# Packing w_in's 64-row remainder of two items into the two row halves of TensorE, in a three-stage kernel on one core

## The chip, the cores and the metric

The kernel runs on one NeuronCore of a Trainium2 chip. The metric is the device time of one execution in microseconds; the kernel before took 1141.08 us (median of three runs, 1140.94 to 1141.94). Engines are named as in the profile: PE multiplies, PEld is its weight loading, DVE, ACT and POOL work element by element, SP issues the DMAs.

## What is computed

Two sequences of 4096 tokens with 192 channels go through a dynamic convolution (per token and head a softmax over 7 taps, applied to the token and the six before it) and then two feed-forward layers over all 8192 tokens:

```python
out = np.einsum('bshk,bskhg->bshg', softmax(weight_gen), windows_of(x))   # -> (8192, 192)

h = x @ w_in                       # 192 -> 2048
g = where(h >= 1, h, where(h <= -1, 0, (h + 1) ** 2 / 4))
x = g @ w_out                      # 2048 -> 192

h = x @ w_in2
g = h - tanh(h)
return g @ w_out2
```

All is float32. To use TensorE at its faster float32r format, each operand is split into a high part, the value rounded to that format, and a low part, the rest; a product is then high x high + low x high + high x low.

## The kernel before

The 8192 tokens are 16 blocks (b) of N = 512, the 2048 hidden channels 16 chunks (f) of P = 128. An **item** (m, b, f) is chunk f of block b in feed-forward layer m (0 or 1): a first product into one PSUM bank h (`item`, L850; contracted over 192 channels), an activation on ACT and DVE (L880 to L901), a cast of the result to its high part gh on ACT (L918) and a low part gl on DVE or POOL (L926), and a second product with w_out's chunk f into the block's accumulators, three items later. `order` (L287) lists the 512 items: first the blocks (0, 0) and (0, 1) interleaved, the second SKEW items behind the first, then (0, 2), then (1, 0) and (1, 1) interleaved, then (0, 3), (1, 2), (0, 4), (1, 3) and so on, one whole block after the other, to (1, 15).

192 channels are 128 + 64. The first 128 fill TensorE's rows; the last 64, called the third part here, fill half of them. Weights come as float32 and are split on the chip (`weights`, L316): per group of two items a load, two steps that take the bits apart (ACT and ACT or POOL), a `join` on DVE (L357), a cast to the high part on ACT (L374) and the low part on DVE or POOL (L378). For w_in such a group is 512 words wide: 2 x 128 columns of the first 128 channels, and 2 x 128 columns of the third part, which is loaded twice, into rows 0 to 63 and again into rows 64 to 127. The activations (tile xt, named a for layer 0, b for layer 1) have the high part of the first 128 channels, their low part, and in a third plane the third part's high in rows 0 to 63 and its low in rows 64 to 127.

**Plain items** (all of the first LANES = 64 items, and the last block): the first product is five full-row matmuls of 512 columns, `mm1` (L860, matmul at L864): high x high, low x high and high x low of the first 128 channels, then w_in's third part, high and low, against the plane that has high and low side by side. The second product is five full-row matmuls (L939 to L946), in the last block a form with the tokens on the other side (L951).

**Paired items** (from item 64 to the last block): `both` (L816) runs the first product of two items and the second product of two earlier ones as 64-row matmuls, always one on rows 0 to 63 beside one on rows 64 to 127 (`chunks`, L782; `second`, L764; `weave`, L793). There the third part needs its high part in both halves; a copy of it is made by ACT (L1038, L1135) or by a further DMA (L701) into tiles x3.

The first items' second product takes the joined weights without splitting, in plain float32 (`whole`, L309; L905 to L912): items 0 to 3 of block (0, 0) and item 0 of block (0, 1), by WHOLE = (4, 1).

The convolution of blocks 0 to 2 ends on PE with transposes and is then split by ACT and DVE (`conv`, L398; hi1 at L625, lo1 at L631). From block 3 on the rows go out to DRAM and come back transposed (`move_rows`, L655; `back`, L686). Between layer 0 and layer 1 `finish1` (L1017) splits a block's result.

No engine's order is written by hand: `Plan.run` (L70) lays every task in time by keys and assumed durations and writes the instructions in that order. The keys' offsets are the constants from L1172 on.

Of the kernel before, what the change touches and what calls it, by code (L numbers as in the profile page):

```python
# [169 lines left out]
def tile_dynconv_moe_moe(  # L170
# [45 lines left out]

    ident = const.tile([P, P], F32, tag="ident", name="ident")
# [9 lines left out]
    win = tiles("win", 2, [P, 4, FF], F32R)  # L227
# [8 lines left out]
    x3_t = {}  # L236

    def x3(s):

        n, k = divmod(s.n, 2)  # L240
        if n not in x3_t:
            x3_t[n] = const.tile([P, 2, N], F32R, tag=f"raw{n}", name=f"x3_{n}")
        return x3_t[n][D1:P, k]

    def third(m, b):

        s = x3_of[m, b]
        return xt_t[s.n][D1:P, b] if m and b < 2 else x3(s)

    def xt_tile(s, name, shape=(P, 3, N), dt=F32R):  # L250
        xt_t[s.n] = const.tile(list(shape), dt, tag=f"xt{s.n}", name=name)
# [5 lines left out]
    def bits(w):  # L257
# [9 lines left out]
        "x3": [4, 5, 6, 7],  # L267
# [20 lines left out]
    for first, second, skew in turns:  # L288
        if first == (1, 0):
            order += [(0, 2, f) for f in range(NF)]  # L290
        order += [(*first, f) for f in range(skew)]
        step = 1 if first == (0, 0) else 2
        for f in range(0, NF, step):
            order += [(*second, f + k) for k in range(step)]
            order += [(*first, skew + f + k) for k in range(step) if skew + f + k < NF]
# [20 lines left out]
    def weights(kind, m, c, lead):  # L316

        key = at[m, 0, 2 * c] - lead + kind * KOFF
        n = 2 * D if kind else 2 * WC
# [10 lines left out]
        def load(e):  # L330
            r = raws[raw.n]
            if kind == 0:
                w = bits_in[m][:, c * WC:(c + 1) * WC]
                return [e.dma_start(r[q], w[k]) for q, k in (
                    ((slice(0, P), slice(0, WC)), slice(0, P)), ((slice(0, D1), slice(WC, None)), slice(P, D)), ((slice(D1, P), slice(WC, None)), slice(P, D)),
                )]
            else:
                return e.dma_start(r[:, 0:n].rearrange("p (f c) two -> p f c two", f=2), bits_out[m][:, 2 * c:2 * c + 2])
# [23 lines left out]
        def pieces():  # L362
            src = value().rearrange("p (a c) -> p a c", a=2)
            if kind == 0:
                cs = slice(c * WC, (c + 1) * WC)
                return [(win[m][:, 0:2, cs], win[m][:, 2:4, cs], src)]
            w = wout[m][:, 2 * c:2 * c + 2, :]

            return [
                (w[:, :, P:2 * P], w[:, :, 0:P], src[:, :, 0:P]),  # L370
                (w[:, :, 2 * P:2 * P + D1], w[:, :, 2 * P + D1:], src[:, :, P:D]),
            ]

        def cast(e):  # L374
            for hi, lo, src in pieces():
                e.copy(hi, src)
# [11 lines left out]
        t = wcast[kind, m, c] = plan.add(on("ACT", 0.09 + 0.43 * k + 0.1 * split), key2, cast, [t], uses=[val])  # L388
# [6 lines left out]
    a_of, b_of, x3_of = {}, {}, {}  # L395
    x3_free = []

    def conv(b, banks, base, gap):  # L398
# [216 lines left out]
        def parts():  # L615

            xtr = X(2).rearrange("p (q h n) -> p q h n", h=2, n=P)
            if b == 0:
                p1r = p1.rearrange("p (q h n) -> p q h n", h=2, n=P)
                sides = p1r[:, :, 0], p1r[:, :, 1]  # L620
            else:
                sides = (p1[:, 0:N // 2].rearrange("p (q n) -> p q n", n=P),) * 2
            return [(slice(0, D1), slice(D1, P), sides[0], xtr[:, :, 0]), (slice(D1, P), slice(0, D1), sides[1], xtr[:, :, 1])]

        def hi1(e):  # L625
            if b == 0:
                xt_tile(xt, f"a_{b}")
            for u, _, p, s in parts():
                e.copy(s[u], p[u])

        def lo1(e):  # L631
            for u, v, p, s in parts():
                e.tensor_tensor(s[v], p[u], s[u].bitcast(F32), op=ALU.subtract)
# [8 lines left out]
        if b == 0:  # L642
            h1 = plan.add(on("ACT", 0.76), last, hi1, [tr1], takes=[xt], uses=second_)
# [3 lines left out]
        else:  # L647
            h0 = plan.add(on("ACT", 0.48), last, hi0, [tr], takes=[xt], uses=first_)
            h1 = plan.add(on("ACT", 0.76), last, hi1, [h0], uses=second_ + [xt])
            l0 = plan.add(on("DVE", 0.60), last, low0, [h0], uses=first_ + [xt])  # L650
            l1 = plan.add(on("DVE", 0.86), last, lo1, [h1], uses=second_ + [xt])
        marks["evac", b] = l1
        xdone[0, b] = [h0, h1, l0, l1]

    def move_rows(b, wg, xw, mem, xt, dep, key, turn):  # L655
# [21 lines left out]
        xs3 = x3_of[0, b] = slot("x3")  # L677
# [8 lines left out]
        def back(e, n, k):  # L686
# [19 lines left out]
        for n, k in ((0, 0), (0, 1), (1, 0), (1, 1)):  # L706
            first = [] if moves else [marks["fin1", b - 1]]
            moves.append(plan.add(
                on("DMA", 1.0), last, lambda e, n=n, k=k: back(e, n, k), [d1 if n else d0] + moves[:1] + first + (x3_free if len(moves) == 1 else []),
                takes=[xs3] if len(moves) == 1 else [] if moves else [xt], uses=[spot] + ([xt] if moves else []), late=3.0,  # L710
# [21 lines left out]
    head, ending, closes = [], [], []  # L732
    lows, apart = slot("xt"), slot("bank", lambda: (0, 1, 6, 7))

    def paired(m, b):

        return b >= MOVED - m and (m, b) != (1, NB - 1)
# [9 lines left out]
    HALVES = [slice(0, D1), slice(D1, P)]  # L747
# [33 lines left out]

    def chunks(lane, m, b, f, h, xs):  # L782

        rs, fs = HALVES[lane], slice(f * P, (f + 1) * P)
        ops = [(0, 0), (2, 0), (0, 1), (1, 2)] + ([(3, 2 + lane)] if f % 2 == lane else [])

        def mm(e, n, k, c):
            x = third(m, b) if c == 3 else xt_t[xs.n][rs, c]
            return e.matmul(ps[h.n], win[m][rs, k, fs], x, start=lane == 0 and n == 0, stop=lane == 1 and n == len(ops) - 1)  # L789

        return [lambda e, n=n, k=k, c=c: mm(e, n, k, c) for n, (k, c) in enumerate(ops)]

# [23 lines left out]
    def both(m, b, f, h0, h1, need):  # L816
# [25 lines left out]
        t = plan.add(on("PE", 0.68), i, one, need + [last[0]] + late2[g0][9], takes=[h0, h1] + opens, uses=[xs, x3_of[m, b]] + rest, late=0.0)  # L842
        t = plan.add(on("PE", 1.365), i, two, [t] + late2[g1][9], uses=[h0, h1, xs, x3_of[m, b]] + both_, late=0.0)
        first = plan.add(on("PE", 0.2265 * n), i, three, [t], uses=[h0, xs, x3_of[m, b]] + both_, late=0.35)
        end = last[0] = plan.add(on("PE", 0.2265 * (10 - n)), i + 1, four, [first], uses=[h1, xs, x3_of[m, b]] + both_, late=0.35)
# [4 lines left out]
    def item(m, b, f, after):  # L850
# [9 lines left out]
        def mm1(e, ns=range(5)):  # L860
            w, xt = win[m], xt_t[xs.n]
            for n in ns:
                k, c = [(0, 0), (2, 0), (0, 1), (1, 2), (3, 2)][n]
                e.matmul(ps[h.n], w[:, k, fs], xt[:, c], start=n == 0, stop=n == (2 if i < 2 else 4))  # L864

        need1 = after + xdone[m, b] + [wdone.get((0, m, f // 2))]
        if i < 2:
            head.append(plan.add(on("PE", 0.46), i - 1.5, lambda e: mm1(e, range(2)), xdone[m, b][:1] + need1[-1:] + head, takes=[h], uses=[xs], late=0.1))
            first = plan.add(on("PE", 0.68), i, lambda e: mm1(e, (3, 4, 2)), need1 + head[:1], uses=[h, xs], late=0.35)
        elif not lanes1(i):  # L870
            first = plan.add(on("PE", 1.135), i, mm1, need1, takes=[h], uses=[xs], late=0.35)
        elif f % 2 == 0:
            h1 = slot("bank", h_banks(m, b))
            first, second = both(m, b, f, h, h1, need1)
# [53 lines left out]
        tlo = plan.add(engines, i, low_part, [thi], takes=[gl], uses=[g], lock=True)  # L928
# [81 lines left out]
    held, thirds = [], []  # L1010
# [6 lines left out]
    def finish1(b, acc, key, t, g=None):  # L1017
# [14 lines left out]
        rl = plan.add(on("DVE", 0.60), key, lambda e: e.tensor_tensor(X(2)[D1:P], M(), X(2)[0:D1].bitcast(F32), op=ALU.subtract), [rh], uses=[s, tm])  # L1032
        marks["fin1", b] = r
        hold(g, [(h1, "gh", 4), (r, "gl", 5), (h0, "gh", 5), (l0, "gl", 6), (rh, "gh", 6), (rl, "gl", 7)])
        xdone[1, b] = [h0, l0, rh, rl]
        if paired(1, b):
            s3 = x3_of[1, b] = slot("x3")
            xdone[1, b].append(plan.add(on("ACT", 0.525), key, lambda e: e.copy(x3(s3), X(2)[0:D1]), [rh] + x3_free, takes=[s3], uses=[s]))  # L1038
# [81 lines left out]
    x3_free += [wdone[kind, 1, c] for kind in range(2) for c in range(NF // 2)]  # L1120
    place = {q: n for n, q in enumerate(streams)}
    for m, b, f in order:
# [6 lines left out]
        if (m, b, f) == (1, 0, 0):  # L1129
            s3 = slot("xt")  # L1130

            def copy3(e, c):
                if c == 0:
                    xt_tile(s3, "thirds")
                e.copy(xt_t[s3.n][D1:P, c], xt_t[b_of[c].n][0:D1, 2])  # L1135

            for c in range(2):
                x3_of[1, c] = s3
                t = plan.add(on("ACT", 0.525), LANES - 7.0, lambda e, c=c: copy3(e, c), [xdone[1, c][2]] + thirds[:1], takes=[] if c else [s3], uses=[b_of[c]] + ([s3] if c else []))
                thirds.append(t)  # L1140
# [8 lines left out]
        if m and b < 2 and lanes1(at[m, b, f]):  # L1149
            dep = dep + [thirds[b]]  # L1150
        if at[m, b, f] == LANES:
            dep = dep + [prev2.get((1, 0)), prev2.get((1, 1))]
# [20 lines left out]
WHOLE = (4, 1)  # L1173
LEAD2 = 4.0
DONE1, DONE2 = 9.0, 11.0
FLEX = 2.0
WARM = 24
VONE = 1
KOFF = 4.0
LOAD1 = 4.0  # L1180
LOWF = 4.0
UNTIL = 3.5
SKEW = 11
LANES = 64
SKEW2 = 8
RAMP, RAMP_UNTIL = 0.5, 48
BASE3, BASE = 40.0, 40.0
PACE = 1.3
LEAD = (4.0, 14.0)
CONV1 = (0.0, 0.5)  # L1190
# [30 lines left out]
```

## Time and profile before

| | us |
|---|---|
| median of three runs | 1141.08 |
| span of the profiled execution | 1138.7 |
| PE busy in it | 1132.1 |
| DVE busy | 974.1 |
| ACT busy | 843.7 |
| POOL busy | 109.1 |

The span runs from the first to the last instruction of the profiled execution; its time outside the span isn't recorded, and the median of the unprofiled runs lies 2.4 us above the span. TensorE's granted clock is 1.0 of full speed in every stretch, that is 2.4 GHz, but for 0.99 in the last 29 us.

How to read it: a matmul's duration in the trace (0.39 us here) is longer than the distance to the next one, since matmuls are pipelined; the distance of two starts is what a matmul costs PE. 64*128 in a row is a matmul on 64 rows, 128*128 one on all rows.

### The profile page before, as it was taken

How to read it: one execution, taken by the hardware profiler on the slowest of the kernel's cores; microseconds unless marked ns; L12 is line 12 of the kernel's file. 1: busy time of each engine (PE TensorE's matmuls, PEld its weight loads, DVE VectorE, ACT ScalarE, POOL GpSimd, SP SyncE). 2: the span in 40 equal slices, each digit the busy share in tenths (PEclk: the TensorE clock that was granted, in tenths of full speed). 3: DMA queues.
4: the chain of work that ended last, by engine and by line, in shares of the span. 5: the costliest groups of instructions: out<-in, count | busy, mean ns of one | idle time of the engine just before them, and what ended most of it. 6: DMA issues, size and time to landing. Idle time of an engine off the chain costs nothing.

```text
span 1138.7 us, 24533 instructions
## 1 busy us (share of the span) xinstructions
PE 1132.1 (99%) x9155; PEld 932.3 (82%) x9155; DVE 974.1 (86%) x1484; ACT 843.7 (74%) x1482; POOL 109.1 (10%) x108
## 2 busy tenths in 40 slices
PE   8999999999999999999999999999999999999998
PEld 6788888888888888888888888888888888888887
DVE  8998998988988989888888988989888888876665
ACT  6989966877768677686776768777686776868654
POOL 5865820000000000000000000000000000000000
PEclk9999999999999999999999999999999999999999
DMA  7603303111120211203011130111202111030000
GB/s 249 211 24 118 97 19 96 28 47 55 34 82 15 68 38 42 69 15 100 10 43 64 19 96 16 51 51 32 81 16 72 35 42 29 16 61 13 4 8 21
DMA packets 102334, 62.27 MB, mean 55 GB/s; under 512 B 63692, under 2 KB 90442, under 8 KB 102216
## 3 DMA queue, kind: packets, MB, share of 16 engines
q1 hardware_dynamic: 101928, 60.52, 19.3%
q8 instruction: 72, 1.18, 0.4%
q14 instruction: 46, 0.38, 0.1%
q10 hardware_dynamic: 288, 0.20, 0.1%
HBM read 44.16 MB, written 16.52 MB: 53 GB/s over the span
## 4 chain that ended last, share of the span: by engine, by line
PE 99%; DVE 0%; ACT 0%; issue 0%; POOL 0%; DVEq 0%; POOLq 0%
PE ps L773 43%; PE ps L789 39%; PE ps L864 8%; PE ps L939 1%; PE ps L945 1%; PE ps L940 1%; PE ps L941 1%; PE ps L946 1%; PE ps L966 1%; PE ps L1105 1%; PE ps L967 0%; PE ps L912 0%; PE ps L911 0%; PE ps L520 0%; DVE gw L896 0%
## 5 line engine op out<-in xcount | busy, mean ns | idle before, releaser
L773 PE MATMUL ps<-gh,wout 64*128 64x512 f32 x2592 | 827.8, 386 | 0.0
L773 PE MATMUL ps<-gl,wout 64*128 64x512 f32 x1728 | 667.0, 386 | 0.0
L773 PEld LDWEIGHTS ps<-gh,wout 64*128 64x128 f32 x2592 | 476.9, 184 | 51.0
L789 PE MATMUL ps<-b,win 64*128 64x512 f32 x1904 | 467.4, 386 | 0.0
L789 PE MATMUL ps<-a,win 64*128 64x512 f32 x1768 | 433.9, 386 | 0.0
L789 PEld LDWEIGHTS ps<-b,win 64*128 64x128 f32 x1904 | 350.3, 184 | 40.0 <-issue 0.4
L918 ACT CAST gh<-g 128x512 fp32r<-128x512 f32 x507 | 311.7, 618 | 60.6 <-DVE g L901 35.3
L789 PEld LDWEIGHTS ps<-a,win 64*128 64x128 f32 x1768 | 325.3, 184 | 36.8
L773 PEld LDWEIGHTS ps<-gl,wout 64*128 64x128 f32 x1728 | 318.0, 184 | 34.0
L926 DVE TENSOR_TENSOR gl<-g,gh 128x512 fp32r<-128x512 f32 x467 | 321.7, 689 | 16.9 <-ACT gh L918 10.4
L900 ACT ACTIVATE g<-ps 128x512 f32<-128x512 f32 x256 | 152.0, 599 | 137.6 <-PE ps L789 124.2
L896 DVE SCALAR_TENSOR_TENSOR g<-ps,g 128x512 f32<-128x512 f32 x251 | 172.0, 687 | 72.1 <-ACT g L890 70.0
L901 DVE TENSOR_TENSOR g<-ps,g 128x512 f32<-128x512 f32 x256 | 171.6, 683 | 59.4 <-ACT g L900 57.5
L884 ACT ACTIVATE g<-ps 128x512 f32<-128x512 f32 x243 | 144.2, 593 | 54.8 <-PE ps L789 52.4
L890 ACT ACTIVATE g<-g 128x512 f32<-128x512 f32 x256 | 161.8, 632 | 7.7 <-DVE g L883 0.2
L481 DVE TENSOR_TENSOR prod<-xw,wg 128x768 f32<-128x768 f32 x84 | 83.4, 993 | 0.0
L789 PE MATMUL ps<-x,win 64*128 64x512 f32 x208 | 80.3, 386 | 0.0
L436 POOL MEMSET xw<- 1x1152 f32 (+1 forms) x4 | 2.9, 732 | 724.8 <-DMA a<-spot 658.2
L560 DVE TENSOR_TENSOR acc<-acc,prod 128x768 f32<-128x768 f32 x70 | 68.4, 977 | 0.0
L864 PE MATMUL ps<-a,win 128*128 128x512 f32 x240 | 61.0, 392 | 1.0 <-ACT a L638 1.0
L926 POOL TENSOR_TENSOR gl<-g,gh 128x512 fp32r<-128x512 f32 x40 | 55.0, 1380 | 24.7 <-ACT gh L918 5.5
L864 PEld LDWEIGHTS ps<-a,win 128*128 128x128 f32 x240 | 44.7, 188 | 12.9 <-ACT a L638 1.2
(131 smaller groups left out, 787.3 us busy)
## 6 DMA issues: line engine op xcount, KB each, us to landing
xw<-in_x_dram SPq DMA_DIRECT2D x13, 960.0 KB, 6.3
spot<-xw SPq DMA_DIRECT2D x104, 96.0 KB, 2.0
raw<-in_moe_w_out_dram SPq DMA_DIRECT2D x16, 384.0 KB, 3.2
a<-spot SPq DMA_DIRECT2D x24, 256.0 KB, 2.9
out_dram<-raw SPq DMA_DIRECT2D x360, 16.0 KB, 1.5
raw<-in_moe_w_in_dram SPq DMA_DIRECT2D x16, 256.0 KB, 3.4
raw<-in_moe_w_in_dram SPq DMA_DIRECT2D x32, 128.0 KB, 4.0
a<-spot SPq DMA_DIRECT2D x24, 128.0 KB, 3.0
```

Source lines behind the costliest of these rows:

```text
L481: return e.tensor_tensor(dst.rearrange("p j (h g) -> p j h g", h=H), xws[xw.n][:, k:k + T, :].rearrange("p j (h g) -> p j h g", h=H), w[:, ...
L560: return e.tensor_tensor(prods[k % 2] if early and k == mine - 1 else acc_sb, acc_sb, prods[k % 2], op=ALU.add)
L773: return e.matmul(to(), w[rs, c:c + P], (GL() if low else GH())[rs], start=f == 0 and lane == 1 and n == 0, stop=f == NF - 1 and lane == 0 ...
L789: return e.matmul(ps[h.n], win[m][rs, k, fs], x, start=lane == 0 and n == 0, stop=lane == 1 and n == len(ops) - 1)
L864: e.matmul(ps[h.n], w[:, k, fs], xt[:, c], start=n == 0, stop=n == (2 if i < 2 else 4))
L884: e.activation(G_(), H_(), AF.Relu, bias=1.0)
L890: t = plan.add(on("ACT", 0.537), i, lambda e: e.activation(G_(), G_(), AF.Square, scale=0.5), [t], uses=[g])
L896: return e.scalar_tensor_tensor(GL() if plain else G_(), H_(), 1.0, G_(), op0=ALU.max, op1=ALU.min)
L900: t = plan.add(on("ACT", 0.49), i, lambda e: e.activation(G_(), H_(), AF.Tanh), [first], takes=[g], uses=[h])
L901: t = plan.add(on("DVE", 0.605), i, lambda e: e.tensor_tensor(G_(), H_(), G_(), op=ALU.subtract), [t], uses=[g, h])
L918: thi = plan.add(on("ACT", 0.527), i, lambda e: e.copy(GH(), G_()), [t], takes=[gh], uses=[g])
L926: return e.tensor_tensor(GL(), G_(), GH().bitcast(F32), op=ALU.subtract)
```

## The change

**The weights.** A group of two items in w_in is now 384 words wide: 2 x 128 columns of the first 128 channels, and 128 columns in which rows 0 to 63 hold the third part of the first item and rows 64 to 127 that of the second. High and low parts lie in `win[m][:, 0, c]` and `win[m][:, 1, c]`. The third part is loaded once.

**The activations.** xt has four planes: high and low of the first 128 channels, and high and low of the third part, each of the two now in both row halves. `hi1` copies three pieces instead of two, POOL makes the second copies for blocks 0 to 2 (`twice`), `back` brings the third part in four transfers instead of three, `finish1` makes two more copies on ACT in place of the one into x3. The x3 tiles go.

**The first product.** Per item it is three full-row steps (WIDE) and three half-row steps (NARROW): high x high, low x high and high x low of the third part, the first item's on rows 0 to 63 and the second's on rows 64 to 127. Plain items are now taken in pairs by `duo`: three full steps of the first item, then the narrow steps of both items in turn, then three full steps of the second. The first pair of all is written apart: two full steps of each item, then for each item the last full step and its own three narrow ones. In the paired items `chunks` takes the same steps, nine per lane and pair as before.

**The rest.** WHOLE becomes (4, 0), so that four items instead of five have a plain float32 second product; the interleaving goes in twos from the start, and the constants of the plan change.

```diff
-    win = tiles("win", 2, [P, 4, FF], F32R)
+    win = tiles("win", 2, [P, 2, NF // 2, 3 * P], F32R)
...
-                    ((slice(0, P), slice(0, WC)), slice(0, P)), ((slice(0, D1), slice(WC, None)), slice(P, D)), ((slice(D1, P), slice(WC, None)), slice(P, D)),
+                    (r[:, 0:WC], w[0:P]), (r[0:D1, WC:n], w[P:D, 0:P]), (r[D1:P, WC:n], w[P:D, P:2 * P]),
...
-            for u, _, p, s in parts():
-                e.copy(s[u], p[u])
+            for rows, h in ((HALVES[0], 0), (HALVES[1], 1), (HALVES[0], 1)):
+                e.copy(at_(2, rows, h), sides()[h])
...
+        def twice(e):
+            r = e.tensor_copy(at_(2, HALVES[1], 0), at_(2, HALVES[0], 0).bitcast(F32))
+            return [r, e.tensor_copy(X(3)[D1:P], X(3)[0:D1].bitcast(F32))]
...
-                rows(xt_[n * D1:(n + 1) * D1, 2, :], d[P:D])
-            if (n, k) == (0, 1):
-                rows(x3(xs3).bitcast(F32), d[P:D])
+                for half_ in HALVES:
+                    rows(xt_[half_, 2 + n, :], d[P:D])
...
+    WIDE, NARROW = [(0, 0), (1, 0), (0, 1)], [(0, 2), (1, 2), (0, 3)]
+
+    def step(e, m, f, h, xs, k, c, rows=slice(0, P), **flags):
+
+        n = 2 * P if c > 1 else f % 2 * P
+        return e.matmul(ps[h.n], win[m][rows, k, f // 2, n:n + P], xt_t[xs.n][rows, c], **flags)
...
-        ops = [(0, 0), (2, 0), (0, 1), (1, 2)] + ([(3, 2 + lane)] if f % 2 == lane else [])
+        ops = WIDE + (NARROW if f % 2 == lane else [])
...
+    def duo(m, b, f, hs, need, x_):
...
+        def narrow(e, ds=range(2), opens=(), ends=()):
+            for n, (k, c) in enumerate(NARROW):
+                for d in ds:
+                    step(e, m, f + d, hs[d], xs, k, c, HALVES[d], start=d in opens and n == 0, stop=d in ends and n == 2)
...
+        if i:
+            t = plan.add(on("PE", 0.68), i, lambda e: wide(e, 0), need + x_[:2], takes=hs[:1], uses=[xs], late=0.1)
+            first = plan.add(on("PE", 0.88), i + 0.1, lambda e: narrow(e, opens=(1,), ends=(0,)), x_ + [t], takes=hs[1:], uses=[hs[0], xs], late=0.35)
+            return first, plan.add(on("PE", 0.68), i + 0.2, lambda e: wide(e, 1, ends=True), [first], uses=[hs[1], xs], late=0.35)
...
-        elif not lanes1(i):
-            first = plan.add(on("PE", 1.135), i, mm1, need1, takes=[h], uses=[xs], late=0.35)
...
+                first, second = duo(m, b, f, [h, h1], after + need1[-1:], xdone[m, b])
...
-WHOLE = (4, 1)
+WHOLE = (4, 0)
...
-SKEW = 11
+SKEW = 14
```

PE before, among the plain items of layer 1: five matmuls of one item's first product (ps_66, ps_67 are banks h), then five of another item's second product (ps_63 is an accumulator).

```order
L864 MATMUL ps_66<-b_736,win_82 128x512 x5
L939 MATMUL ps_63<-gh_99,wout_84 128x512
L940 MATMUL ps_63<-gh_99,wout_84 128x512
L941 MATMUL ps_63<-gh_99,wout_84 128x512
L945 MATMUL ps_63<-gl_14_612,wout_84 128x512
L946 MATMUL ps_63<-gl_14_612,wout_84 128x512
L864 MATMUL ps_67<-b_736,win_82 128x512 x5
```

PE after, among the plain items of block (0, 2): one pair's first product and one second product. Where a row says x4, three are full-row steps and one is a narrow one.

```order
L770 MATMUL ps_65<-a_892,win_81 128x512 x4
L770 MATMUL ps_66<-a_892,win_81 128x512
L770 MATMUL ps_65<-a_892,win_81 128x512
L770 MATMUL ps_66<-a_892,win_81 128x512
L770 MATMUL ps_65<-a_892,win_81 128x512
L770 MATMUL ps_66<-a_892,win_81 128x512 x4
L946 MATMUL ps_64<-gh_99,wout_83 128x512
L947 MATMUL ps_64<-gh_99,wout_83 128x512
L948 MATMUL ps_64<-gh_99,wout_83 128x512
L952 MATMUL ps_64<-gl_5_390,wout_83 128x512
L953 MATMUL ps_64<-gl_5_390,wout_83 128x512
```

Two first products now stand together, the two second products behind them; between the full-row steps lie six half-row ones.

PE before, the first four items, up to the first plain float32 second product:

```order
L864 MATMUL ps_65<-a_213,win_81 128x512 x2
L864 MATMUL ps_66<-a_213,win_81 128x512 x2
L864 MATMUL ps_65<-a_213,win_81 128x512 x3
L864 MATMUL ps_66<-a_213,win_81 128x512 x3
L864 MATMUL ps_68<-a_213,win_81 128x512 x5
L864 MATMUL ps_67<-a_213,win_81 128x512 x5
L910 LDWEIGHTS whole
```

And after, in the same place:

```order
L770 MATMUL ps_65<-a_216,win_81 128x512 x2
L770 MATMUL ps_68<-a_216,win_81 128x512 x2
L770 MATMUL ps_65<-a_216,win_81 128x512 x4
L770 MATMUL ps_68<-a_216,win_81 128x512 x4
L770 MATMUL ps_67<-a_216,win_81 128x512 x4
L770 MATMUL ps_66<-a_216,win_81 128x512
L770 MATMUL ps_67<-a_216,win_81 128x512
L770 MATMUL ps_66<-a_216,win_81 128x512
L770 MATMUL ps_67<-a_216,win_81 128x512
L770 MATMUL ps_66<-a_216,win_81 128x512 x4
L917 LDWEIGHTS whole
```

The first pair (ps_65, ps_68) has one full and three narrow steps in each x4 row, and its narrow steps don't alternate; the second pair (ps_67, ps_66) has the common form.

POOL after, at the start of the program, behind the convolution's taps of block 0: the two copies of `twice` for block 0 stand between the first steps on the weights' bits.

```order
L465 TENSOR_TENSOR taps_153<-xw_91,wg_77 128x768 x3
L339 TENSOR_SCALAR raw_87<-raw_87 128x384
L621 CAST a_216<-a_216 64x2x128
L622 CAST a_216<-a_216 64x512
L339 TENSOR_SCALAR raw_88<-raw_88 128x384
```

Before, a low part of w_in (L379) stood first behind the same taps, and POOL wrote nothing of a.

## Rows read from the trace of the kernel before

**Rows 1.** Page, part 1: busy us, share of the span, instructions.

```profile
PE 1132.1 (99%) x9155; PEld 932.3 (82%) x9155; DVE 974.1 (86%) x1484; ACT 843.7 (74%) x1482; POOL 109.1 (10%) x108
```

**Rows 2.** Page, part 4: chain that ended last, share of the span by line.

```profile
PE ps L773 43%; PE ps L789 39%; PE ps L864 8%; PE ps L939 1%; PE ps L945 1%; PE ps L940 1%; PE ps L941 1%; PE ps L946 1%; PE ps L966 1%; PE ps L1105 1%; PE ps L967 0%; PE ps L912 0%; PE ps L911 0%; PE ps L520 0%; DVE gw L896 0%
```

**Rows 3.** Waits of PE: what waited for what, us, times, longest.

```profile
PE ps L864 <- ACT a L638: 1.0, 1, 1.0
PE ps L911 <- DVE whole L360: 0.5, 1, 0.5
```

**Rows 4.** Timeline of PE, plain items: start, us, engine, line, operation.

```profile
159.58 1.30 PE L864 MATMUL ps<-b,win 128*128 128x512 f32 x5
```

**Rows 5.** Busy time by stretch: length, engines (instructions), granted clock, DMA share, GB/s.

```profile
163.07:1093.47 930.40, 930.40 (x8209) 768.74 (x8208) 795.02 (x1216) 680.33 (x1162) 2.93 (x4) 1.00 0.17 44
...
20.07:52.00 31.93, 31.93 (x118) 20.20 (x119) 31.24 (x51) 29.52 (x63) 27.30 (x31) 1.00 0.69 221
```

**Rows 6.** Timeline of PE, from the plain items into the paired ones.

```profile
161.85 1.29 PE L864 MATMUL ps<-b,win 128*128 128x512 f32 x5
163.07 0.49 PE L789 MATMUL ps<-b,win 64*128 64x512 f32 x1
163.08 0.49 PE L773 MATMUL ps<-gh,wout 64*128 64x512 f32 x1
163.41 0.39 PE L789 MATMUL ps<-b,win 64*128 64x512 f32 x1
...
165.03 0.39 PE L789 MATMUL ps<-b,win 64*128 64x512 f32 x1
```

**Rows 7.** Timeline of PE, the plain float32 item of block (0, 1).

```profile
49.58 0.39 PE L910 MATMUL ps<-whole 128*128 128x512 bf16 x1
49.81 1.02 PE L911 MATMUL ps<-gw,whole 128*128 128x512 f32 x2
50.76 1.07 PE L912 MATMUL ps<-gw,whole 128*64 128x512 f32 x2
51.77 1.42 PE L864 MATMUL ps<-a,win 128*128 128x512 f32 x5
```

**Rows 8.** Timeline of PE, out of the paired items into the last block.

```profile
1093.24 0.39 PE L773 MATMUL ps<-gl,wout 64*128 64x512 f32 x1
...
1093.56 0.50 PE L939 MATMUL ps<-gh,wout 128*128 128x512 f32 x1
1093.89 0.40 PE L940 MATMUL ps<-gh,wout 128*128 128x512 f32 x1
...
1094.82 1.32 PE L864 MATMUL ps<-b,win 128*128 128x512 f32 x5
```

**Rows 9.** Timeline of ACT at the start.

```profile
13.01 0.74 ACT L629 CAST a<-ps 64x256 fp32r<-64x256 f32 x2
13.78 0.59 ACT L638 CAST a<-ps 128x512 fp32r<-128x512 f32 x1
```

**Rows 10.** Timeline of PE at the start; in brackets the idle time before, and its releaser.

```profile
14.42 4.88 PE L864 MATMUL ps<-a,win 128*128 128x512 f32 x20 [1.01 <-ACT a L638]
...
20.07 0.70 PE L911 MATMUL ps<-gw,whole 128*128 128x512 f32 x1 [0.54 <-DVE whole L360]
```

**Rows 11.** Groups of POOL by shape: busy us, mean ns of one | idle before, releasers.

```profile
L379 POOL TENSOR_TENSOR win<-val,win 128x512 fp32r<-128x512 f32 x10 | 12.9, 1290 | 7.1 <-DVE a L633 3.6 <-DVE g L896 2.8 <-ACT g L890 0.4
...
L379 POOL TENSOR_TENSOR wout<-val,wout 128x128 fp32r<-128x128 f32 x10 | 6.1, 607 | 0.0
```

**Rows 12.** Timeline of DVE at the start.

```profile
14.08 0.86 DVE L633 TENSOR_TENSOR a<-ps,a 64x256 fp32r<-64x256 f32 x2
14.97 0.69 DVE L641 TENSOR_TENSOR a<-ps,a 128x512 fp32r<-128x512 f32 x1
```

**Rows 13.** Groups by shape: the copy of the third part for paired items, ACT.

```profile
L1038 ACT CAST x<-b 64x512 fp32r<-64x512 f32 x13 | 8.0, 618 | 0.4
```

More of the change, by code (lines that the diff above doesn't have):

```diff
@@ L234, in tile_dynconv_moe_moe, with xt_tile @@
     xt_t = {}
[L236 to L250, printed above, removed]
+    def xt_tile(s, name, shape=(P, 4, N), dt=F32R):
         xt_t[s.n] = const.tile(list(shape), dt, tag=f"xt{s.n}", name=name)
@@ L291, in tile_dynconv_moe_moe @@
         order += [(*first, f) for f in range(skew)]
[L292 to L295, printed above, removed]
+        for f in range(0, NF, 2):
+            order += [(*second, f + k) for k in range(2)]
+            order += [(*first, skew + f + k) for k in range(2) if skew + f + k < NF]
     for m, b in streams[5:]:
@@ L374, in cast @@
         def cast(e):
-            for hi, lo, src in pieces():
-                e.copy(hi, src)
+            if kind == 0:
+                return e.copy(win[m][:, 0, c], value())
+            return e.copy(wout[m][:, 2 * c:2 * c + 2, P:P + D], value().rearrange("p (a c) -> p a c", a=2))
         def rest(e):
@@ L642, in conv @@
         if b == 0:
-            h1 = plan.add(on("ACT", 0.76), last, hi1, [tr1], takes=[xt], uses=second_)
+            h1 = plan.add(on("ACT", 1.12), last, hi1, [tr1], takes=[xt], uses=second_)
             h0 = plan.add(on("ACT", 0.50), last, hi0, [tr, h1], uses=first_ + [xt])
@@ L708, in move_rows @@
             moves.append(plan.add(
-                on("DMA", 1.0), last, lambda e, n=n, k=k: back(e, n, k), [d1 if n else d0] + moves[:1] + first + (x3_free if len(moves) == 1 else []),
-                takes=[xs3] if len(moves) == 1 else [] if moves else [xt], uses=[spot] + ([xt] if moves else []), late=3.0,
+                on("DMA", 1.0), last, lambda e, n=n, k=k: back(e, n, k), [d1 if n else d0] + moves[:1] + first,
+                takes=[] if moves else [xt], uses=[spot] + ([xt] if moves else []), late=3.0,
             ))
@@ L731, in tile_dynconv_moe_moe @@
     partner = {}
-    head, ending, closes = [], [], []
+    ending, closes = [], []
     lows, apart = slot("xt"), slot("bank", lambda: (0, 1, 6, 7))
-    def paired(m, b):
-        return b >= MOVED - m and (m, b) != (1, NB - 1)
     def lanes1(i):
@@ L841, in both @@
         rest = [s for s in both_ if s not in opens]
[L842 to L845, printed above, removed]
+        t = plan.add(on("PE", 0.68), i, one, need + [last[0]] + late2[g0][9], takes=[h0, h1] + opens, uses=[xs] + rest, late=0.0)
+        t = plan.add(on("PE", 1.365), i, two, [t] + late2[g1][9], uses=[h0, h1, xs] + both_, late=0.0)
+        first = plan.add(on("PE", 0.2265 * n), i, three, [t], uses=[h0, xs] + both_, late=0.35)
+        end = last[0] = plan.add(on("PE", 0.2265 * (10 - n)), i + 1, four, [first], uses=[h1, xs] + both_, late=0.35)
         prev2[late2[g1][:2]] = end
@@ L1128, in tile_dynconv_moe_moe @@
                 conv(b, (2, 3), at[0, b, 0] - (BASE3 if b == 3 else BASE), 1.1)
[L1129 to L1140, printed above, removed]
         if f:
```

111 lines of the change are left out of this document (54 added, 57 removed).

## Prediction

> **What bounds the kernel now.** I read the busy times first: PE is busy 1132.1 of 1138.7 us [rows 1]. A busy PE need not be a full one, so the chain of work that ended last comes next: its costliest three lines are PE's, L773, L789 and L864, and together they hold 90% of the span [rows 2]. Third, who PE waited for: after the warming there are two waits in the whole run, 1.0 us before the first multiplication and 0.5 us for the first decoded w_out group [rows 3]. So from 20 us on whatever lengthens or shortens PE's own row of instructions goes straight into the time.
>
> What PE's time is made of is read from its timeline. I call a *step* one 512-column matmul over all 128 rows, or two 64-row ones side by side. Five steps of L864 and five of the second product repeat every 2.27 us (159.58 to 161.85) [rows 4, 6], so a step is 0.227 us. In the long middle stage 8,208 half-row matmuls (the row counts one full one that reaches in) take 930.40 us [rows 5], 0.2267 us for each pair, and the two halves start 0.01 us or less apart [rows 6]: half-row matmuls on different halves do run side by side, at the same price per step.
>
> **What the change removes from PE.** Outside the middle stage, which keeps its 9.5 steps an item, there are 32 pairs before and 8 pairs after it. A pair's first product goes from 10 steps to 6 full and 3 paired ones: one step less. The first pair is written apart (L800 to L806 of the new code): its three narrow steps run on one half only, for each of its items, so it takes 12 steps, not 9. That is 40 - 3 = 37 steps, 37 x 0.2267 = **8.4 us** less.
>
> One item fewer runs its second product in plain fp32 (WHOLE from (4, 1) to (4, 0)). In the trace this item takes PE from 49.58 to 51.77, and the five steps behind it last 0.12 us longer than usual (1.42 for 1.30) [rows 4, 7]: 2.3 us for what takes five steps, 1.13 us, otherwise. **1.2 us** less.
>
> **What it adds to PE.** Each pair now goes from full-row matmuls to half-row ones and back. The program before does this twice in all, into the middle stage and out of it; the new order has 84 such changes (two for each of 39 pairs, four in the first, two for the middle stage), so 82 more. Their price stands in two places. Into halves: five steps of L864 begin at 161.85, the next should begin at 162.98, but begins at 163.07, and the one behind it at 163.41 where 163.21 was due; by 165.03, 13 steps on, 3.18 us have gone where 2.95 were due [rows 6]. That is 0.20 us at once and 0.23 in all. Out of halves: 1093.24 to 1093.89 for two steps, 0.65 for 0.45, and 1.58 us to 1094.82 for six, where 1.36 were due [rows 8]: 0.20 and 0.22. About half of it lies ahead of the first new matmul (0.09), the rest between it and the next (0.11). In a new pair only three steps stand between two changes, so I take 0.21, little more than the part paid at once: 82 x 0.21 = **17.2 us** more, with 16.4 (0.20) and 18.9 (0.23) as bounds.
>
> The Trainium skill speaks against this change: "TensorEngine Tiling (Array Packing)", Key Properties, says that a change of the tiling mode, not of the tile alone, drains TensorE. It gives no price; by the rule all 82 changes pay one, which is the sum below, and without it the second rival stands. The trace agrees as far as it goes: both changes that it has cost 0.20 us.
>
> **The start.** The copy of x's upper parts by ACT (hi1) now has three pieces. Two take 0.77 us from 13.01 to the next copy at 13.78 [rows 9], so a third puts the first matmul from 14.42 [rows 10] to 14.80: 0.4 us later. On the other side PE stood idle for 0.54 us before L911 at 20.07 [rows 10]; the first four items now end later by their changes and solo steps, and use this up. Together **-0.1 us**, with -0.5 (the third copy hidden) and +0.4 (the idle time comes back) as bounds. The second item of the first pair also waits for POOL's two new copies (L621, L622), 256 and 512 wide on 64 rows. The nearest POOL rows are 0.61 us for 128 wide and 1.29 for 512 [rows 11], so the two take 1.2 to 2.6 us. DVE's subtraction ahead of them ends at 14.94 now [rows 12], 15.3 with the third copy, so they end between 16.5 and 17.9. PE can go on with the first item when DVE's next one ends (15.66 + 0.38 = 16.0) [rows 12], and has then two full steps, three solo ones and three changes before it needs the copies: 16.0 + 5 x 0.23 + 3 x 0.2 = 17.8. I take nothing, and 0.1 as the bound.
>
> **What costs nothing.** Decoding w_in 384 words wide shortens three engines' work by a quarter per group; PE doesn't wait for it after 20 us [rows 3]. ACT's two extra copies per block in finish1, less the copy for x3 that goes, are one of about 0.62 us [rows 13] in the 69 us of a block of both layers (32 items of 9.5 steps), under an ACT that is busy 680 of 930 us in the middle stage [rows 5]; the cover is the 16 items between the end of a block in layer 0 and its use in layer 1. If it were gone, 0.6 us a block would show, 9 us in all. The rows brought back from DRAM are six transfers instead of five on SP's queue; the DMA share there is 0.17 [rows 5].
>
> **The sum:** -8.4 - 1.2 + 17.2 - 0.1 = +7.5 us. On the profiled execution's span that is 1138.7 + 7.5 = 1146.2; the median of the runs (1141.1) is 2.4 us above that span, so **1148.6 us**. With a change at 0.20 and the start at -0.5 it is 6.3 more (1147.4), with 0.23 and +0.4 it is 9.7 more (1150.8).
>
> **The rivals.**
>
> *Only one change of a pair costs.* If the way back to full rows were hidden, 41 x 0.21 = 8.6 stands in the sum for 17.2: 1141.1 - 8.4 - 1.2 + 8.6 - 0.1 = 1140.0, no measurable change. For it: each direction has a single row, and both rows lie where the program's stages change too. Against it: both measure 0.20, although PE meets different waits there. Chance 0.08.
>
> *Changes cost nothing, the step saved is the result.* 1141.1 - 8.4 - 1.2 - 0.1 = 1131.4, faster. The price decides: below (8.4 + 1.2 + 0.1) / 82 = 0.12 us per change the sum turns negative. The 0.20 would then have to be the start of a new stage and not of a new shape. Chance 0.06.
>
> *A new wait on top.* A pair's two items now finish within 0.7 us of each other, and DVE is busy 31.24 of 31.93 us between 20 and 52 us [rows 5], while more items of block 0 come before block 1 joins (SKEW 14 for 11). If every pair there, 31.93 / 4.54 = 7, waits for one more DVE operation of 0.69 us [rows 12], that is 4.8 on top: 1153.4. Against it: a slower PE gives DVE more time. Chance 0.13.
>
> *The narrow steps don't run side by side.* Then 39 x 3 x 0.2267 = 26.5 us on top, 1175.1. The middle stage shows the opposite [rows 6]. Chance 0.02.
>
> **How the numbers follow.** The forecast itself has 0.71. A measurement of this kernel can tell about 0.2%, 2.3 us, from no change. Slower by more than that: 0.71 + 0.13 + 0.02 = 0.86; within it 0.08; faster 0.06. The range runs from 1145, a little under the low bound for changes that fall on a wait that is there anyway, to 1154, which takes in the new wait; outside it lie 0.16 for the rivals on the fast side and for solo narrow steps, and little else.
>
> **What would show it.** In the trace of the changed kernel: in each pair 0.32 us or so from the last full step to the first narrow one and 0.33 to the next, the same on the way back, 82 times; a pair's first product at about 2.45 us for 2.27; the start of the middle stage some 6 us later, the middle stage itself at 930.4, and the last block 1.5 us longer. It is wrong if the distances at a change are below 0.3 us, if PE shows new waits between 20 and 52 us, or if the middle stage's length moves.

## The result: 8.2 us slower

The changed kernel takes 1149.68 us (median of 4 runs, 1149.55 to 1150.38) where the kernel before, run beside it, takes 1141.51 (1140.94 to 1142.33): a ratio of 1.0072, with a 95% interval from 1.0058 to 1.0087. The forecast was 1148.6, in a range from 1145 to 1154.

Part 1 of the page of the kernel after (busy us, share of the span, instructions) answers to [rows 1], and the first line of part 4, the chain that ended last by engine, goes with [rows 2]:

```profile
PE 1140.9 (99%) x9235; PEld 1001.8 (87%) x9235; DVE 966.2 (84%) x1488; ACT 855.5 (75%) x1482; POOL 110.6 (10%) x116
...
PE 98%; POOL 1%; DVE 0%; ACT 0%; issue 0%; POOLq 0%; DVEq 0%; ACTq 0%
```

PE is still the bound, and is busy for 8.8 us more. The 37 steps that went (8.4 us) don't show: something longer came. Where it came is read from the windows of the kernel after, one for each stage (length, then busy time of PE, PEld, DVE, ACT, POOL with instructions, granted clock, DMA share, GB/s). The first stage runs from the first L770 matmul to the first half-row matmul of the lanes, the middle one from there to the first full-row matmul behind them:

```profile
15.01:170.86 155.85, 155.33 (x693) 104.95 (x693) 138.85 (x209) 131.06 (x255) 101.13 (x100) 1.00 0.29 90
170.86:1101.35 930.49, 930.49 (x8210) 850.64 (x8209) 789.52 (x1214) 695.56 (x1175) 2.94 (x4) 1.00 0.18 46
1101.35:1144.60 43.25, 43.04 (x248) 34.63 (x246) 26.95 (x46) 22.38 (x40) 0.00 (x0) 1.00 0.06 10
```

Before, the first stage went from 14.42 [rows 10] to 163.07 [rows 6] and the middle one to 1093.56 [rows 8]; the last block counts here to the start of PE's last matmul, 1134.99 before and 1144.12 after.

| us | before | after | difference | forecast |
|---|---|---|---|---|
| first matmul starts | 14.42 | 15.01 | +0.59 | +0.4 |
| first stage | 148.65 | 155.85 | +7.20 | +5.6 |
| middle stage | 930.49 | 930.49 | 0.00 | 0 |
| last block | 41.43 | 42.77 | +1.34 | +1.5 |
| span | 1138.7 | 1147.9 | +9.2 | +7.5 |

The forecast column is the prediction's sum put to its stages: 29 of the 37 steps (-6.6), the float32 item (-1.2), 66 of the 82 changes (+13.9) and the idle time before L911 (-0.5) in the first stage; 8 steps (-1.8) and 16 changes (+3.4) in the last block. The spans differ by 1 us more than the medians. The profiled execution of before is one of its shorter ones: the runs of it beside the first experiments had spans of 1138.6 to 1140.1.

PE's timeline of the kernel after, in one pair of block (0, 1) (start, us, operation), shows the changes themselves:

```profile
51.29 0.39 PE L953 MATMUL ps<-gl,wout 128*128 128x512 f32 x1
51.60 1.85 PE L770 MATMUL ps<-a,win 64*128 64x512 f32 x9
...
54.44 1.74 PE L770 MATMUL ps<-a,win 128*128 128x512 f32 x9
56.11 0.50 PE L946 MATMUL ps<-gh,wout 128*128 128x512 f32 x1
56.45 0.40 PE L947 MATMUL ps<-gh,wout 128*128 128x512 f32 x1
```

From 51.29 to 51.60 are 0.31 us into the halves, from 56.11 to 56.45 are 0.34 us behind the way back; without a change both would be 0.23. In the 77 changes after 25 us the distances into halves are 0.318 and then 0.335 us, those out of halves 0.326 and then 0.337 (medians): 0.200 us too much into halves and 0.211 out of them, nowhere over 0.227. All 84 changes are in the trace.

The PE busy column doesn't show them as a wait, since the modelled ends of the matmuls cover the gap. The weight loads do. The first line is PEld's waits of the kernel after (us, times, longest), the others are its timeline in a pair of block (1, 0):

```profile
PEld ps L770 <- issue: 29.0, 81, 0.4
```

```profile
134.68 0.53 PEld L770 LDWEIGHTS ps<-b,win 64*128 64x128 f32 x6 [0.35 <-issue]
135.57 0.53 PEld L770 LDWEIGHTS ps<-b,win 128*128 128x128 f32 x3 [0.37 <-issue]
136.14 0.19 PEld L946 LDWEIGHTS ps<-gh,wout 128*128 128x128 f32 x1
```

The load unit stands idle for 0.35 us ahead of the six half-row loads and for 0.37 us ahead of the full-row ones. In a steady row a load of the next weights starts together with the matmul before it and runs beside it. At a change it starts only 0.32 us after that matmul's start (134.36 to 134.68), in the same moment as the first matmul of the new shape. That is the other side of the 0.2 us.

One new thing is in PE's row. Its waits in the kernel after have a line that before lacks [rows 3], and its timeline shows the place:

```profile
PE ps L952 <- POOL gl L933: 0.5, 1, 0.5
```

```profile
82.42 0.39 PE L948 MATMUL ps<-gh,wout 128*128 128x512 f32 x1
82.81 0.50 PE L952 MATMUL ps<-gl,wout 128*128 128x512 f32 x1
83.15 0.40 PE L953 MATMUL ps<-gl,wout 128*128 128x512 f32 x1
...
83.86 0.40 PE L948 MATMUL ps<-gh,wout 128*128 128x512 f32 x1
84.77 0.50 PE L952 MATMUL ps<-gl,wout 128*128 128x512 f32 x1 [0.52 <-POOL gl L933]
85.11 0.40 PE L953 MATMUL ps<-gl,wout 128*128 128x512 f32 x1
```

L952 multiplies the low part of g, which POOL works out here. From 83.86 to 85.11 are 1.25 us for two steps, 0.80 over their due 0.45; from 82.42 to 83.15 it is 0.28. With two smaller ones, from 77.48 on (0.18 too much) and from 86.03 on (0.24), that is 1.5 us, about the part of the first stage that the forecast lacks (1.6).

### The profile page after: what moved, and what is told of

The parts are those of the page before. It is cut to its first block, busy times and chain, and to the rows that moved or that the text cites. A ratio compares the mean times of both kernels' runs of the same rounds, so it can differ in the third digit from the quotient of the medians.

```text
span 1147.9 us, 24739 instructions
## 1 busy us (share of the span) xinstructions
PE 1140.9 (99%) x9235; PEld 1001.8 (87%) x9235; DVE 966.2 (84%) x1488; ACT 855.5 (75%) x1482; POOL 110.6 (10%) x116
## 4 chain that ended last, share of the span: by engine, by line
PE 98%; POOL 1%; DVE 0%; ACT 0%; issue 0%; POOLq 0%; DVEq 0%; ACTq 0%
PE ps L770 47%; PE ps L756 43%; PE ps L952 1%; PE ps L946 1%; PE ps L953 1%; PE ps L947 1%; PE ps L948 1%; PE ps L973 1%; PE ps L1111 1%; POOL gl L933 0%; PE ps L974 0%; PE ps L504 0%; PE ps L919 0%; PE ps L918 0%; DVE acc L544 0%
## 5 line engine op out<-in xcount | busy, mean ns | idle before, releaser
L770 PE MATMUL ps<-b,win 64*128 64x512 f32 (+1 forms) x2208 | 521.7, 389 | 0.0
L770 PE MATMUL ps<-a,win 64*128 64x512 f32 (+1 forms) x2160 | 510.1, 390 | 1.4 <-ACT a L627 1.4
L770 PEld LDWEIGHTS ps<-b,win 64*128 64x128 f32 (+1 forms) x2208 | 395.1, 184 | 34.4 <-issue 11.7
L770 PEld LDWEIGHTS ps<-a,win 64*128 64x128 f32 (+1 forms) x2160 | 381.7, 184 | 43.7 <-issue 17.2
L908 DVE TENSOR_TENSOR g<-ps,g 128x512 f32<-128x512 f32 x256 | 173.9, 685 | 78.0 <-ACT g L907 75.8
L933 POOL TENSOR_TENSOR gl<-g,gh 128x512 fp32r<-128x512 f32 x41 | 58.6, 1434 | 25.0 <-ACT gh L925 6.5
L952 PE MATMUL ps<-gl,wout 128*128 128x512 f32 x60 | 23.9, 398 | 0.5 <-POOL gl L933 0.5
L946 PE MATMUL ps<-gh,wout 128*128 128x512 f32 x60 | 24.0, 399 | 0.0
L947 PE MATMUL ps<-gh,wout 128*128 128x512 f32 x60 | 23.5, 392 | 0.0
```

What stands on the lines that cost most here:

```text
L770: return e.matmul(ps[h.n], win[m][rows, k, f // 2, n:n + P], xt_t[xs.n][rows, c], **flags)
L908: t = plan.add(on("DVE", 0.605), i, lambda e: e.tensor_tensor(G_(), H_(), G_(), op=ALU.subtract), [t], uses=[g, h])
L933: return e.tensor_tensor(GL(), G_(), GH().bitcast(F32), op=ALU.subtract)
L946: e.matmul(p0, w[:, P:2 * P], GH(), start=a, stop=False)
```

## The experiments

The theory (T1): every change between full-row and half-row matmuls costs PE about 0.2 us, and the time is the changes less the steps saved. The rivals: the changes are cheap and the time went into new waits of the re-planned first stage; or the price belongs to the start of a stage, not to a change of shape.

**1. The changes taken out of the new kernel.** Each two narrow steps side by side become one on full rows. All three of a pair go into the first item's bank, so that bank gets the third parts of both items and the second item's bank gets none; the number of steps stays:

```diff
+            d = ds[0]
             for n, (k, c) in enumerate(NARROW):
-                for d in ds:
-                    step(e, m, f + d, hs[d], xs, k, c, HALVES[d], start=d in opens and n == 0, stop=d in ends and n == 2)
+                step(e, m, f + d, hs[d], xs, k, c, start=False, stop=n == 2)
...
-                step(e, m, f + d, hs[d], xs, k, c, start=(k, c) == WIDE[0] and not ends, stop=ends and (k, c) == WIDE[-1])
+                step(e, m, f + d, hs[d], xs, k, c, start=(k, c) == WIDE[0], stop=ends and (k, c) == WIDE[-1])
```

> The changed kernel with every narrow slot of the plain pairs as one full-row matmul: the same number of steps in the same order, but 2 changes between full and half rows instead of 84. It leaves something out: both items' third parts go into the first item's bank alone. If a change of shape costs 0.20 to 0.21 us, 82 of them are 16.4 to 17.2 us and this takes about 1133 us; the middle stage stays at 930.4 us, the last block loses 3.3 us and the first stage 13. If the changes cost nothing and something else of the change made it slow, it stays at 1149.7. If DVE, ACT or POOL can't follow the faster PE in the first stage, only the last block's 3.3 us and a part of the rest come: 1136 to 1146.

Measured: 1140.68 us (1140.32 to 1141.41), ratio to before 0.9998 (0.9988 to 1.0007). The last block falls from 42.77 to 39.24 us, 3.53 for 16 changes, or 0.22 each: T1. But the first stage gives back only 5.6 of the 13 us that its 66 changes should be worth. PE's waits and the windows of this kernel:

```profile
PE ps L952 <- POOL gl L933: 4.3, 7, 1.2
...
PE ps L946 <- ACT gh L925: 0.7, 1, 0.7
PE ps L770 <- DVE g L903: 0.6, 2, 0.4
PE ps L948 <- POOL wout L364: 0.4, 1, 0.4
```

```profile
15.28:165.53 150.25, 144.24 (x601) 108.79 (x601) 136.54 (x208) 129.69 (x254) 102.79 (x100) 1.00 0.29 93
165.53:1096.01 930.48, 930.48 (x8209) 768.74 (x8208) 790.13 (x1216) 695.14 (x1175) 2.93 (x4) 1.00 0.18 46
```

PE is idle for 6.0 of 150.25 us, and L952 waits for POOL's low parts seven times. Due were 148.65 - 29 x 0.2267 - 1.2 = 140.9 us, so 9.3 us are missing, more than the idle time. PE's timeline at the second of the waits of L952 shows why:

```profile
74.10 0.39 PE L948 MATMUL ps<-gh,wout 128*128 128x512 f32 x1
75.53 0.50 PE L952 MATMUL ps<-gl,wout 128*128 128x512 f32 x1 [1.04 <-POOL gl L933]
75.87 0.39 PE L953 MATMUL ps<-gl,wout 128*128 128x512 f32 x1
```

Two distances of 0.2267 have become 1.43 and 0.34 us, 1.3 us more for an idle time of 1.04. From 34 us to the end of the stage 31 distances are over 0.26 us, and together they are 10.1 us over the steady step (0.6 in the kernel before). So what the change saves PE in this stage is eaten by the work that feeds it. With this plan a kernel whose changes cost nothing would not be 10 us faster than before, but equal to it.

**2. The same in the last block alone** (the lines above, under `(m, b) == (1, NB - 1)`). There PE waits for nobody.

> The same in the last block alone, 8 pairs (it too adds both items' third parts to one bank there): 68 changes instead of 84. Price per change 0.205: 16 x 0.205 = 3.3 us less, 1146.4. If the price belongs to the first stage, with its decoding, and not to the changes: 1149.7.

Measured: 1145.94 us (1145.74 to 1146.49), ratio 1.0046 (1.0031 to 1.0061). That is 3.74 us under the kernel after, for 16 changes: 0.23 each by medians, and 0.22 by the stage (42.77 to 39.24).

**3. and 4. The changes put into the kernel before.** The fifth step of a plain item runs on rows 0 to 63 alone; the number of steps stays. First in all plain items:

```diff
-                e.matmul(ps[h.n], w[:, k, fs], xt[:, c], start=n == 0, ...)
+                rs = slice(0, D1) if n == 4 else slice(0, P)
+                e.matmul(ps[h.n], w[rs, k, fs], xt[rs, c], start=n == 0, ...)
```

> The kernel before with the fifth step of each plain item on rows 0 to 63 alone. It leaves out low x low of the third part. The number of steps stays, 158 changes between full and half rows are added. Price per change 0.205: 32.4 us more, 1173.9. If a change costs only at the start of a stage, or when the work behind it is new, nothing: 1141.5. If the way back is free: 16 us more, 1157.7.

Then in the last block alone (`n == 4 and (m, b) == (1, NB - 1)`):

> The same in the last block's 16 items alone (low x low of the third part left out there): 32 changes more than before. By 0.205 each 6.6 us more, 1148.1. A price that isn't per change would not go down to a fifth of the other run's.

Measured: 1172.01 us (1171.67 to 1172.18) with 158 more changes, ratio 1.0274 (1.0258 to 1.0289), and 1146.99 (1146.62 to 1147.97) with 32, ratio 1.0056 (1.0041 to 1.0071). Against the runs of before beside them (1140.95) these are 31.1 and 6.0 us: 0.197 and 0.19 us for each change. In PE's timeline of the first of the two:

```profile
157.10 1.50 PE L865 MATMUL ps<-b,win 128*128 128x512 f32 x5
158.53 0.50 PE L946 MATMUL ps<-gl,wout 128*128 128x512 f32 x1
158.86 0.39 PE L947 MATMUL ps<-gl,wout 128*128 128x512 f32 x1
```

1.76 us for six steps, where six times 0.2267 are 1.36: 0.40 for the way there and back. No data, order, weights layout or stage of the new kernel is in these two, so the price belongs to the change of shape.

**5. More changes in the new kernel.** Each narrow step stands between full ones, 240 changes for 84, the steps being the same:

```diff
+            def mixed(e):
+                for n, (k, c) in enumerate(NARROW):
+                    if n:
+                        wide(e, 0, WIDE[n:n + 1])
+                    for d in range(2):
+                        step(e, m, f + d, hs[d], xs, k, c, HALVES[d], ...)
```

> The changed kernel with the narrow slots of each pair (but the first pair's) set between the full steps: the same steps, 6 changes a pair instead of 2, 240 in all instead of 84. If every change costs the same 0.205, whatever stands between two of them, 156 x 0.205 = 32 us more: 1181.7. If the price is paid once for a group, because the array has then to be filled anew, less than half of that.

Measured: 1181.18 us (two runs, 1181.12 and 1181.25), ratio 1.0352 (1.0331 to 1.0372): 31.5 us over the kernel after for 156 changes, 0.202 each. PEld's idle time grows with the count, from 81 times to 237:

```profile
PEld ps L770 <- issue: 61.5, 237, 0.4
```

**6. The start.** hi1's third copy for block 0 becomes a task of its own, behind the copy that the first matmul waits for.

```diff
-            for rows, h in ((HALVES[0], 0), (HALVES[1], 1), (HALVES[0], 1)):
+            for rows, h in ((HALVES[0], 0), (HALVES[1], 1), (HALVES[0], 1))[:2 if b == 0 else 3]:
...
+            h2 = plan.add(on("ACT", 0.37), last, lambda e: e.copy(at_(2, HALVES[0], 1), sides()[1]), [h0], uses=second_ + [xt])
```

> The changed kernel with hi1's third copy for block 0 behind the copy that the first matmul waits for. The first matmul should come 0.37 us earlier (14.6 for 15.0). As PE has no idle time left before the first plain float32 product at 21.48, that should come to the end: 1149.3. If another wait in the first 6 us takes it up (the joined w_out, POOL's second copies), L918 stays at 21.5 and the time at 1149.7.

Measured: 1154.28 us (1153.25 to 1155.72), ratio 1.0120 (1.0103 to 1.0137), so 4.6 us worse than the kernel after. The first matmul does start earlier, at 14.44 for 15.01. But the planner then put the join of w_out's first group at 22.87 on DVE, where it stood at 17.91. PE's timeline of this kernel (its L919 is L918 of the kernel after):

```profile
14.44 6.41 PE L771 MATMUL ps<-a,win 128*128 128x512 f32 x24 [1.01 <-ACT a L627]
20.68 0.39 PE L918 MATMUL ps<-whole 128*128 128x512 bf16 x1
23.47 1.13 PE L919 MATMUL ps<-gw,whole 128*128 128x512 f32 x2 [2.39 <-DVE whole L345]
```

It is no clean test of the start. It shows that one task more re-orders the first stage, and that such a new order can cost 4 us.

**7. and 8. Is it the plan's prices?** The planner orders the first stage by durations that it is given for the pairs' tasks. Experiment 1 again, with the lower durations that it now has (0.68 for 0.88, 0.91 for 1.1), and the kernel after with durations that hold the price of the changes (1.1 for 0.88, 1.32 for 1.1):

> The full-row kernel without changes of shape in the plain pairs (1140.7 us; both items' third parts in one bank), its plan made with the durations that its steps now have (0.68 for the narrow group instead of 0.88). In the first stage of that kernel PE waits for POOL's low parts and others, some 8 us. If those waits come from an order that was made for a slower PE, they go: 1133 to 1135. If DVE, ACT and POOL have no more room there, it stays within 2 us of 1140.7.

> The changed kernel with two changes of shape instead of one in the plan's duration of the narrow group (1.1 for 0.88; 1.32 for 1.1 in the first pair). Nothing is computed otherwise, only the order is made anew. If the 1.5 us that PE waits for POOL's low parts between 77 and 87 us come from the plan's wrong price, 1148.2; if the order hardly moves or new waits come, 1149.7 or more. The 84 changes stay at 0.20 each.

Measured: 1140.69 us (1139.92 to 1141.0), ratio 0.9993 (0.9983 to 1.0002), and 1150.66 (1150.22 to 1151.33), ratio 1.0084 (1.0069 to 1.0099). Neither gains. PE's largest wait after 20 us stays the one for POOL's low parts, in the first of them and in the second:

```profile
PE ps L952 <- POOL gl L933: 3.8, 6, 1.2
```

```profile
PE ps L952 <- POOL gl L933: 1.4, 2, 1.0
```

So the waits of experiment 1 don't come from these durations in the plan. Which of DVE, ACT and POOL would have to be relieved was not tried.

**9. to 12. Earlier lanes.** The middle stage has no changes. If it begins earlier, pairs and their changes go. In the kernel after LANES = 48 (UNTIL = 2.5) leaves out 16 changes and LANES = 32 (UNTIL = 1.5) leaves out 32; LANES = 48 was also tried in the kernel before, alone and with the float32 item fewer (WHOLE = (4, 0)).

```diff
-UNTIL = 3.5
+UNTIL = 2.5
...
-LANES = 64
+LANES = 48
```

> The changed kernel with the paired form from item 48 on instead of 64, and POOL's part of the low halves ending at item 40: 8 pairs fewer in the form with changes, 16 changes less. By 0.205 each 3.3 us less, 1146.4. The rival: the paired form passes its order through POOL, which is busy with the weights' decoding there, so that PE waits for POOL; then the gain is lost in new waits of PE between items 48 and 64.

> The changed kernel with the paired form from item 32 on instead of 64, POOL's part of the low halves ending at item 24: 32 changes fewer. By 0.205 each 6.6 us less, 1143.1 (the run from item 48 on gave 2.9 of the 3.3 us that 16 changes cost). The rival: the weights of layer 1 are decoded between items 28 and 60, on POOL too, through which the paired form passes its order; then PE waits there and the gain is less, or turns into a loss.

> The kernel before with its paired form from item 48 on instead of 64, POOL's part of the low halves ending at item 40; nothing of the change is in it. Eight pairs go from 10 steps of first product to 9 without any change of shape more: 8 x 0.2267 = 1.8 us less, 1139.5. The rival: new waits in the first stage, as the changed kernel had them when its paired form began at item 32.

> The same with four plain float32 items instead of five, the one edit of the change that takes work from PE without a change of shape. In the prediction's sum it is worth 1.2 us: 1138.3 with both, and faster than before by 0.26%. If the fifth plain item was there because the decoded low part of w_out's first group comes too late without it, PE waits near 45 to 50 us and the gain is lost.

| | us | ratio to before | 95% |
|---|---|---|---|
| after, LANES 48 | 1146.75 | 1.0057 | 1.0042 to 1.0072 |
| after, LANES 32 | 1153.64 | 1.0111 | 1.0096 to 1.0126 |
| before, LANES 48 | 1144.62 | 1.0029 | 1.0018 to 1.0039 |
| before, LANES 48, WHOLE (4, 0) | 1146.88 | 1.0050 | 1.0036 to 1.0063 |

The first gains 2.9 us on the kernel after (3.2 were due for 16 changes at 0.2). The second is 4.0 us slower than the kernel after, the third and fourth are 3.5 and 5.7 us slower than before beside them (1141.14). PE's waits in the second, third and fourth, in this order, name the cause: the engines that feed PE don't keep up when the lanes come early.

```profile
PE ps L770 <- DVE g L903: 3.1, 4, 2.0
...
PE ps L770 <- DVE val L345: 0.6, 1, 0.6
PE ps L770 <- POOLq L739: 0.6, 2, 0.5
```

```profile
PE ps L789 <- DVE g L901: 1.4, 2, 0.9
PE ps L789 <- DVE val L360: 1.2, 1, 1.2
```

```profile
PE ps L789 <- DVE g L901: 3.6, 1, 3.6
```

As in experiment 1 they cost more than their idle time: in the third kernel the distances over 0.26 us add up to 5.1 us over the steady step, where the kernel before has 0.6. In the fourth something else comes on top. Behind the idle time of 3.64 us (150.60 to 154.63 from one matmul to the next) the granted clock is 0.50 of full speed from 153.95 to 160.77, that is 1.2 GHz, and a step takes 0.427 us there. That trace is of an execution of 1148.25 us, 1.4 above the median of this kernel, so it is not a picture of the 5.7 us alone.

No kernel of this study is measurably faster than the one before.

## Why the prediction was right, and where it was not

**The price of a change** (82 x 0.21 = 17.2) held. It was read from the only two places that before has [rows 6, 8]; five runs that add or take away changes give 0.19 to 0.23 us each, whether they are 16, 32, 156 or 158, in the old program or the new one (LANES = 48, which moves more than the changes, gives 0.18). The last block, where nothing else moved, gives -8 x 0.2267 + 16 x p = 1.34, so p = 0.197. The Trainium skill ("TensorEngine Tiling (Array Packing)", Key Properties) says that a change of the tiling mode drains TensorE. The 0.200 and 0.211 us lost at the changes agree with it; what happens in TensorE in that time no trace here shows.

**The first rival** (only one direction costs) fell: 0.200 into halves and 0.211 out of them. **The last rival** (narrow steps not side by side) fell: in the pair of block (1, 0) above, 12 matmuls of the first product run from 133.91 to 136.37:

```profile
133.91 2.62 PE L770 MATMUL ps<-b,win 128*128 128x512 f32 x12
136.37 0.40 PE L946 MATMUL ps<-gh,wout 128*128 128x512 f32 x1
```

These are 2.46 us, as foretold (2.45): nine steps and two changes.

**The second rival** (changes cost nothing) fell by its condition, but it also had a wrong price. It took all of the 8.4 + 1.2 us as gain, 1131.4 us; with the changes out the kernel runs at 1140.7. The step that failed there is "from 20 us on whatever lengthens or shortens PE's own row of instructions goes straight into the time": it holds for lengthening (experiments 3 and 5), and was read from the trace of a PE with more to do. Taken out of PE's row in the first stage, the time comes back as waits, above all for POOL's low parts. The forecast used the same saving of 8.4 + 1.2 us without asking whether the feeders had room for it, and came out right because the changes made PE slower than before, so that it stayed the bound: so far it was luck. By the same token 0.12 us per change isn't the point from which the change would pay; below that it would be about even. That is argued from experiment 1, not run.

**The new wait** (third rival) came in part. Its place was put at 20 to 52 us and on DVE, at 4.8 us. DVE has room there now, 27.93 of 32.00 us busy in the kernel after, for [rows 5]:

```profile
20.00:52.00 32.00, 32.00 (x134) 18.30 (x132) 27.93 (x45) 29.30 (x63) 28.42 (x32) 1.00 0.50 160
```

The waits stand between 77 and 87 us, are for POOL, and come to 1.5 us. That is the one term of size that the sum lacked. Why POOL is late just there is seen but not tested: four of its low parts take 7.86 us there, 1.97 each, where the usual one takes 1.30.

**The start** was put at -0.1. The third copy costs what was worked out, 0.40 us, and the two POOL copies take 0.39 and 0.61 us, below the bracket of 1.2 to 2.6. ACT's and POOL's timeline of the kernel after:

```profile
13.21 1.14 ACT L615 CAST a<-ps 64x256 fp32r<-64x256 f32 x3 [0.56 <-PE ps L504]
14.38 0.59 ACT L627 CAST a<-ps 128x512 fp32r<-128x512 f32 x1
```

```profile
14.01 0.39 POOL L621 CAST a<-a 64x256 fp32r<-64x256 f32 x1
15.30 0.61 POOL L622 CAST a<-a 64x512 fp32r<-64x512 f32 x1 [0.90 <-DVE a L618]
```

1.17 us from the first copy to the next, for 0.77 [rows 9]; POOL is through at 15.91, ahead of PE's need. The bracket came from rows of subtractions with two inputs [rows 11]; these are copies, and the trace of before has none on POOL. The rest of the 0.59 us, 0.19, is a start of ACT's copies at 13.21 for 13.01; the last section shows that starts differ by more than that between programs that are the same up to there. The idle time before L911 [rows 10] is gone, as foretold: PE's next multiplications follow without a gap at 21.26 and 21.48.

**What costs nothing** did, in the middle stage: 930.49 us before and after, with ACT's busy time up from 680 to 696 us [rows 5]. In the first stage it did as long as PE was slow; experiment 1, with a PE that has less to do, has the waits.

## What to carry to other kernels

Count how often an instruction stream changes between matmuls on all rows and on row halves, and price each change from a place where the old trace has one: here it is 0.2 us, nearly one step of 512 columns, so a pair that saves one step must not pay two changes. Gather the half-row work into long stretches, as the middle stage does. And a saving on the bounding engine is worth no more than the slack of the engines behind it: work out, stage by stage, who is late when the bound gets faster, before a rival is priced.

## What the runs showed of the hardware that was not expected

- The price is nearly the same in both directions (0.200 us into halves, 0.211 out) and that of one change does not grow with their number: 0.19 to 0.23 us for 16 to 158 of them.
- The second part of the price, 0.34 us instead of 0.23 from the first matmul behind the change to the second, is not peculiar to a change. It also stands behind a wait: 84.77 to 85.11 in the kernel after, 75.53 to 75.87 in experiment 1. These two waits cost 0.80 and 1.31 us, about 0.28 more than the idle time that the profile shows for them (0.52 and 1.04). Whether a wait and a change are late for one reason was not tested.
- It does not show as PE's waiting: PE reads 155.33 us busy of 155.85. The sign of it is the load unit's idle time by "issue", 0.35 to 0.37 us at a change (29.0 us in 81 waits).
- The first matmul of programs with the same code at the start begins at 14.42 and 14.43 us in two of them (the kernel before and experiment 4) and at 15.14 and 15.34 in two others (experiments 11 and 3): 0.7 to 0.9 us of a difference of two spans may be of that sort.
